# A second layer over pairs of blocks in seven products instead of eight, on one Trainium2 core

## The chip, the core and the metric

The kernel runs on one core of one Trainium2 chip. A core has five engines, each with an instruction queue of its own: TensorE (PE; loading a matmul's weights is recorded apart as PEld), VectorE (DVE), ScalarE (ACT), GpSimd (POOL) and SyncE (SP, which here only issues DMAs). The engines meet by semaphores. Each queue is worked in program order, so a waiting instruction holds everything behind it on its engine. The metric is the device time in microseconds, as the median of several runs.

## What is computed

```
x       = inputs x       (4, 6144, 256), f_logit the same shape, lower_bound (256,)
f       = lb + (1 - lb) * sigmoid(f_logit)
h[t]    = f[t] * h[t-1] + (1 - f[t]) * x[t]        # a scan over 6144 steps, h = y[t]
h1, h2  = y @ w1, y @ w2                           # 256 -> 1024
out     = maximum(h1, h2) @ w_out                  # 1024 -> 256, 24576 tokens
```

The kernel writes `maximum(h1, h2)` as `h1 + relu(h2 - h1)`. So the first layer is one product with `wd = w2 - w1` and a relu, and `h1 @ w_out` becomes `y @ w13` with `w13 = w1 @ w_out` made once. (The factor 1 - lb is taken out of the scan and put into `wd` and `w13`.)

## The kernel before

**Tiles.** The 24,576 tokens are cut into 48 blocks of 512 tokens (`TB`). The first four chunks hold one block each, the other 22 (chunks 4 to 25) two blocks (`CH` = 1024 tokens). D = 256 is two groups of 128 partitions (`KC` = 2), DFF = 1024 is eight (`FC` = 8).

**Getting data in.** From chunk 4 on, `fetch` (line 98, POOL) casts 1024 tokens of `f_logit` and of `x` from fp32 to bf16 into one of two DRAM scratches per tensor. `cross` (line 153, SP) then reads each scratch through a DMA transpose into `fT` or `xT` in SBUF, so that channels lie on partitions. The cast into a scratch waits until the transpose that last read that scratch has landed: f's waits for f's transpose, x's for x's. Chunks 1 to 3 are cast into SBUF and turned by TensorE instead (line 180). The very first block is loaded as fp32.

**The work of a block.** `gate(j)`: one sigmoid on ACT over 128x1024 (line 190). `scan_steps(j)`: two decays (line 209), one multiply (line 220) and two scans (line 233) on DVE. `first_layer(j, fc)`: two matmuls with 512 moving columns into one PSUM bank (line 381), then one relu of 128x512 on ACT (line 389). `second_layer(j, slot)`: for each of four token groups, two matmuls with `y` as weights and eight with `rt` as weights, 256 moving columns each (line 410), 40 matmuls to a block. DVE copies each pair of groups out of PSUM (line 430), and SP stores the block (line 433). The token groups are every fourth token, so the weights are read with a step of four elements.

**The order.** It is written out by hand. In iteration `j` of the main loop, eight slots hold `first_layer(j, fc)` and a part of `second_layer(j - 1, fc)` by turns, the gate and the scans of block j + 1 between them. `ahead` issues the transposes of a chunk when the loop is three blocks before it (`LEAD_CROSS`), and its casts seven blocks before. The gate of block j + 1 stands in iteration j, so chunk 5 (blocks 6 and 7) is first read by ACT in iteration 5.

Of the kernel before, what the change touches and what calls it, by code (L numbers as in the profile page):

```python
# [14 lines left out]
P = 128  # L15
# [3 lines left out]
def kernel(  # L19
# [18 lines left out]
    CH = 1024  # L38
    assert S % CH == 0
# [16 lines left out]
    def by_xbar(c, s):  # L56
        return c >= 4
# [6 lines left out]
    natpool = ctx.enter_context(tc.tile_pool(name="nat", bufs=6))  # L64
    inpool = ctx.enter_context(tc.tile_pool(name="inp", bufs=5))
    midpool = ctx.enter_context(tc.tile_pool(name="mid", bufs=2))
    ypool = ctx.enter_context(tc.tile_pool(name="ypool", bufs=4))
    rpool = ctx.enter_context(tc.tile_pool(name="rpool", bufs=2 * FC + 4))
    opool = ctx.enter_context(tc.tile_pool(name="opool", bufs=4))
    ps_t = ctx.enter_context(  # L70
        tc.tile_pool(name="ps_t", bufs=2, space=bass.MemoryType.PSUM)
    )
    ps_d = ctx.enter_context(
        tc.tile_pool(name="ps_d", bufs=3, space=bass.MemoryType.PSUM)
    )
    ps_o = ctx.enter_context(
        tc.tile_pool(name="ps_o", bufs=3, space=bass.MemoryType.PSUM)
# [4 lines left out]
        [dram.tile([CH, D], BF16, name=f"scr{s}_{q}") for q in range(NSCR)]  # L82
        for s in range(2)
    ]
    uses = [0, 0]
# [5 lines left out]
    def fetch(c):  # L91
        b, t0, nt, _ = chunks[c]
        for s in range(2):
            src = srcs[s][b, t0 : t0 + nt, :]
            if by_xbar(c, s):
                scr = scratch[s][uses[s] % NSCR]
                uses[s] += 1
                nc.gpsimd.dma_start(  # L98
                    out=scr[0:nt, :].rearrange("(p i) d -> p (i d)", p=P),
                    in_=src.rearrange("(p i) d -> p (i d)", p=P),  # L100
                )
                held[c, s] = scr
            else:
                nat = natpool.tile([P, CH // P, D], BF16, name=("fn", "xn")[s])
                nc.gpsimd.dma_start(
                    out=nat[:, 0 : nt // P, :].rearrange(
                        "p (k i) d -> p k (i d)", i=TB // P
                    ),
                    in_=src.rearrange(
                        "(k p i) d -> p k (i d)", p=P, i=TB // P  # L110
                    ),
                )
                held[c, s] = nat
# [3 lines left out]
    def fetch_first(k):  # L117
        nt = TB // 2
        for s in range(2):
            raw = const.tile([P, nt // P, D], FP32, name=f"raw{k}{s}")  # L120
            nc.sync.dma_start(  # L121
                out=raw[:],
                in_=srcs[s][0, k * nt : (k + 1) * nt, :].rearrange(
                    "(p i) d -> p i d", p=P
                ),
            )
            raws[k, s] = raw

    def first_bf16(k, s, copy):
        raw = raws[k, s]  # L130
        nat = const.tile([P, raw.shape[1], D], BF16, name=f"nat{k}{s}")
        copy(out=nat[:], in_=raw[:])
        raws[k, s] = nat

    def first_turn(k):
        nt = TB // 2
        for s in range(2):
            dst = ps_t.tile([P, KC, nt // P, P], BF16, name="tT")
# [9 lines left out]
    def cross(c):  # L148
        nt = chunks[c][2]
        for s in range(2):  # L150
            if by_xbar(c, s):
                dst = inpool.tile([P, KC, CH], BF16, name=("fT", "xT")[s])
                nc.sync.dma_start_transpose(  # L153
                    out=dst[:, :, 0:nt], in_=held[c, s][0:nt, :]
                )
                held[c, s] = dst

    def turn_steps(j):
        b, t0, nb, c, o = blocks[j]
        steps = []  # L160
        for s in range(2):
            if by_xbar(c, s):
                turned[j, s] = held[c, s][:, :, o : o + nb]
                continue
            dst = ps_t.tile([P, KC, TB], BF16, name="tT")
            ns = nb // P
            turned[j, s] = dst[:, :, 0:nb].rearrange("p k (i m) -> p k m i", i=ns)
            for q in range(ns):
                for h in range(KC):
# [3 lines left out]
                            held[c, s][:, o // P + q, h * P : (h + 1) * P],  # L173
# [9 lines left out]

    us = {}

    def gate(j):
        nb = blocks[j][2]
        u = midpool.tile([P, KC, TB], BF16, name="u")
        fT = turned[j, 0]
        nc.scalar.activation(  # L190
            out=like(u[:, :, 0:nb], fT), in_=fT, func=AF.Sigmoid, scale=-1.0
        )
        us[j] = u
# [6 lines left out]
    def scan_steps(j):  # L200
        b, t0, nb, c, o = blocks[j]
        u = us[j]
        ff = midpool.tile([P, KC, TB], BF16, name="ff")
        v = midpool.tile([P, KC, TB], BF16, name="v")
        y = ypool.tile([P, KC, TB], BF16, name="y")
        ys[j] = y

        def decay(h):
            nc.vector.tensor_scalar(  # L209
                out=ff[:, h, 0:nb],  # L210
                in0=u[:, h, 0:nb],
                scalar1=nom[:, h : h + 1],
                scalar2=1.0,
                op0=ALU.mult,
                op1=ALU.add,
            )

        def drive():
            xT = turned[j, 1]
            nc.vector.tensor_tensor(  # L220
                out=like(v[:, :, 0:nb], xT),
                in0=like(u[:, :, 0:nb], xT),
                in1=xT,
                op=ALU.mult,
            )

        def scan(h):
            if t0 == 0:
                init = 0.0
            else:  # L230
                pn = blocks[j - 1][2]
                init = ys[j - 1][:, h, pn - 1 : pn]
            nc.vector.tensor_tensor_scan(  # L233
                out=y[:, h, 0:nb],
                data0=ff[:, h, 0:nb],
                data1=v[:, h, 0:nb],
                initial=init,
                op0=ALU.mult,
                op1=ALU.add,
            )  # L240

        return [
            lambda: decay(0),
            lambda: decay(1),
            drive,
            lambda: scan(0),
            lambda: scan(1),
        ]

    first = {}  # L250

    def first_recurrence(k):
        nt = TB // 2
        cols = slice(k * nt, (k + 1) * nt)
        if k == 0:
            for t in ("u", "ff", "v"):
                first[t] = midpool.tile([P, KC, TB], BF16, name=t)
            ys[0] = ypool.tile([P, KC, TB], BF16, name="y")
        u, ff, v, y = (*(first[t] for t in ("u", "ff", "v")), ys[0])
        fT, xT = raws[k, 0], raws[k, 1]  # L260
        nc.scalar.activation(
            out=like(u[:, :, cols], fT), in_=fT, func=AF.Sigmoid, scale=-1.0
        )
        for h in range(KC):
# [7 lines left out]
            )  # L272
        nc.vector.tensor_tensor(
            out=like(v[:, :, cols], xT), in0=like(u[:, :, cols], xT), in1=xT,
            op=ALU.mult,
        )
        for h in range(KC):
# [13 lines left out]

    ident_f = const.tile([P, P], FP32)
# [8 lines left out]
    wdf = wpool.tile([P, KC, DFF], FP32)  # L301
    wd = wpool.tile([P, KC, DFF], BF16)
    w1T = wpool.tile([P, FC, D], BF16)
    w13 = wpool.tile([P, KC, D], BF16)
    NG = 2
    NQ = FC // NG
    w1n = [wpool.tile([P, KC, NQ * P], FP32, name=f"w1n{g}") for g in range(NG)]
    w2n = [wpool.tile([P, KC, NQ * P], FP32, name=f"w2n{g}") for g in range(NG)]
# [3 lines left out]

    def fcs(w, kc, g):
        return w[:, kc, g * NQ * P : (g + 1) * NQ * P].rearrange(
            "p (q m) -> p q m", q=NQ
        )
# [12 lines left out]
    def make_wd(fc, n):  # L329
        g, r = divmod(fc, NQ)  # L330
        qs = slice(r, r + n)
        cols = slice(fc * P, (fc + n) * P)
        nc.vector.tensor_tensor(  # L333
            out=wdf[:, :, cols].rearrange("p kc (q m) -> p kc q m", q=n),
# [4 lines left out]
        for kc in range(KC):  # L339
            if g == 0:  # L340
                nc.scalar.mul(wd[:, kc, cols], wdf[:, kc, cols], om[:, kc : kc + 1])  # L341
            else:
                nc.vector.tensor_scalar_mul(
                    out=wd[:, kc, cols], in0=wdf[:, kc, cols], scalar1=om[:, kc : kc + 1]
                )

    def turn_w1(k):
        g, r = divmod(k, NQ // 2)
        pt = ps_o.tile([P, KC, 2, P], FP32, name="psO")
# [11 lines left out]
    def make_w13():  # L361
        for kc in range(KC):
            psw = ps_o.tile([P, 2, D], FP32, name="psO")
# [9 lines left out]

    rts = {}

    def first_layer(j, fc):
        nb = blocks[j][2]
        y = ys[j]
        dT = ps_d.tile([P, TB], FP32, name="dT")
        for kc in range(KC):  # L380
            nc.tensor.matmul(  # L381
                dT[:, 0:nb],
                lhsT=wd[:, kc, fc * P : (fc + 1) * P],
                rhs=y[:, kc, 0:nb],
# [3 lines left out]
        rt = rpool.tile([P, TB], BF16, name="rt")  # L388
        nc.scalar.activation(out=rt[:, 0:nb], in_=dT[:, 0:nb], func=AF.Relu)  # L389
        rts[j, fc] = rt  # L390
# [3 lines left out]
    def second_layer(j, slot):  # L394
        b, t0, nb, c, o = blocks[j]
        ns = nb // P
# [3 lines left out]
        for k in range(slot * total // FC, (slot + 1) * total // FC):  # L400
            i, s = divmod(k, n)
            g, r = divmod(i, 2)
            if s == 0 and (r == 0 or j == NBLK - 1):
                acc["ps"] = ps_o.tile([P, 2, D], FP32, name="psO")
# [3 lines left out]
            left = y[:, s, i:nb:ns] if s < KC else rts[j, s - KC][:, i:nb:ns]  # L408
            right = w13[:, s, :] if s < KC else wob[:, s - KC, :]
# [8 lines left out]
            if j == NBLK - 1 and s == n - 1:  # L418
# [3 lines left out]
                r0 = b * S + t0  # L422
                (nc.sync if r else nc.scalar).dma_start(
                    out=out[r0 : r0 + nb, :].rearrange("(p n) d -> p n d", p=P)[
                        :, i : i + 1, :
# [21 lines left out]
    with tc.manual_schedule():  # L447
# [60 lines left out]
        if steps:  # L508
            gate(3)
# [62 lines left out]
```

## Time and profile before

| | us |
|---|---|
| Median of 3 runs (lowest, highest) | 400.92 (400.88, 401.1) |
| Span of the profiled execution | 428.3 |
| PE busy | 392.8 (92%) |
| PE's weight loads busy | 296.8 (69%) |
| ACT busy | 268.5 (63%) |
| DVE busy | 248.7 (58%) |
| POOL busy | 26.4 (6%) |
| Cast of f into scratch 0 or 1, median from issue to landing | 7.5 or 7.9 |
| Cast of x into scratch 0 or 1, the same | 12.4 or 13.6 |
| Store of a block (512 KB), the same | 4.8 |
| ACT idle before a gate until an f transpose had landed | 35.5 over 15 waits |
| PE idle before a first-layer matmul until a relu was done | 19.5 over 11 waits |

A time in the profile is that of one execution, the profiled one, which took about 27 us more than the runs that were timed. Busy is the time in which an engine has at least one instruction in work; instructions of one engine overlap at their ends, so the sum of their durations is larger. A matmul's recorded duration runs on after the next one has begun: the distance from start to start is what it costs. "Idle before" is the engine's idle time just in front of a group of instructions, with what ended it.

### The profile page before, as it was taken

To read this page: it belongs to the slowest core of one execution; us is meant where nothing else is said; L and a number is where in the kernel's file an instruction comes from. 1 tells how busy PE (TensorE), PEld (TensorE's weight loads), DVE (VectorE), ACT (ScalarE), POOL (GpSimd) and SP (SyncE) were. 2 spreads that over 40 slices of the span, in tenths; PEclk is the share of its full clock that TensorE was granted. 3 is DMA by queue.
4 is the path that set the end of the run, shared out by engine and by line. 5 is a ranking of instruction groups with operands and counts; after the bars stand their busy time and mean duration, and the time that the engine had idled before them with its cause. 6 is when DMAs were issued, how large, how long until landed. Compare 5 with 4: busy or idle time off the path is not lost.

```text
span 428.3 us, 6970 instructions
## 1 busy us (share of the span) xinstructions
PE 392.8 (92%) x2744; PEld 296.8 (69%) x2792; DVE 248.7 (58%) x359; ACT 268.5 (63%) x447; POOL 26.4 (6%) x58
## 2 busy tenths in 40 slices
PE   3999979798789999998997899999998999999996
PEld 1677756576557777776775577767676777777775
DVE  5785637455357566564653557657547656567551
ACT  3656656557366676675673666756657676776762
POOL 1400000000000000000000000000000000000000
PEclk9999999999989999999999699999999999999999
DMA  7999999999999999999998999999999999998112
GB/s 245 222 220 198 123 157 141 137 169 252 81 240 226 119 239 233 112 248 168 183 237 75 218 158 186 250 145 170 219 131 231 226 216 164 268 157 179 79 69 100
DMA packets 103377, 77.01 MB, mean 180 GB/s; under 512 B 93552, under 2 KB 94064, under 8 KB 102640
## 3 DMA queue, kind: packets, MB, share of 16 engines
q1 hardware_dynamic: 100512, 51.13, 66.7%
q0 software_dynamic: 2544, 25.17, 36.1%
q8 instruction: 22, 0.36, 0.4%
q10 hardware_dynamic: 288, 0.26, 0.2%
q14 instruction: 11, 0.09, 0.1%
HBM read 53.48 MB, written 48.23 MB: 237 GB/s over the span
## 4 chain that ended last, share of the span: by engine, by line
PE 46%; DMA 34%; SPq 15%; ACT 3%; DVE 1%; issue 1%; ACTq 0%
PE psO L410 25%; DMA fT<-scr_0_90 20%; PE dT L381 19%; SPq L153 13%; DMA fT<-scr_1_91 12%; ACT u L190 2%; DMA w1n_110<-in_moe_w_dram 2%; SPq L433 1%; PE psO L352 1%; ACT rt L389 1%; PE tT L180 1%; PE psO L365 0%; SPq L121 0%; DVE osb L430 0%; DVE y L233 0%
## 5 line engine op out<-in xcount | busy, mean ns | idle before, releaser
L389 ACT ACTIVATE rt<-dT 128x512 bf16<-128x512 f32 x384 | 219.2, 598 | 104.1 <-PE dT L381 100.0
L381 PE MATMUL dT<-y,wd 128*128 128x512 bf16 x720 | 219.5, 384 | 21.3 <-ACT rt L389 19.5
L410 PE MATMUL psO<-wob,rt 128*128 128x256 bf16 x1536 | 230.7, 274 | 2.7 <-issue 0.4
L410 PEld LDWEIGHTS <-rt 128*128 128x128 bf16 x1536 | 170.7, 114 | 41.4 <-issue 1.1
L233 DVE TENSOR_TENSOR_SCAN y<-ff,y,v 128x512 bf16<-128x512 bf16 x88 | 107.9, 1268 | 0.1
L430 DVE COPY osb<-psO 128x512 f32<-128x512 f32 x94 | 64.7, 690 | 59.0 <-PE psO L410 58.9
L381 PEld LDWEIGHTS <-wd 128*128 128x128 bf16 x768 | 75.8, 99 | 33.2 <-issue 24.6
L209 DVE TENSOR_SCALAR ff<-u,nom 128x512 bf16<-128x512 bf16 x94 | 29.0, 351 | 105.0 <-ACT u L190 105.0
L410 PE MATMUL psO<-w_109,y 128*128 128x256 bf16 x384 | 74.0, 275 | 0.0
L410 PEld LDWEIGHTS <-y 128*128 128x128 bf16 x384 | 43.4, 113 | 42.6 <-issue 3.5
L190 ACT ACTIVATE u<-fT 128x1024 bf16<-128x1024 bf16 x44 | 46.4, 1054 | 35.5 <-DMA fT<-scr_1_91 18.2
L220 DVE TENSOR_TENSOR v<-u,xT 128x1024 bf16<-128x1024 bf16 x44 | 30.3, 688 | 3.8 <-DMA xT<-scr_0_92 1.8
L98 POOL DMA_DIRECT2D scr_0_90<-in_f_logit_dram x11 | 5.4, 493 | 149.7 <-DMA fT<-scr_0_90 149.7
L98 POOL DMA_DIRECT2D scr_1_91<-in_f_logit_dram x11 | 5.3, 486 | 148.8 <-DMA fT<-scr_1_91 148.1
L233 DVE TENSOR_TENSOR_SCAN y<-ff,v 128x512 bf16<-128x512 bf16 x6 | 7.0, 1208 | 0.0
L98 POOL DMA_DIRECT2D scr_0_92<-in_x_dram x11 | 5.4, 488 | 18.7 <-DMA xT<-scr_0_92 16.9
L98 POOL DMA_DIRECT2D scr_1_93<-in_x_dram x11 | 5.3, 486 | 15.7 <-DMA xT<-scr_1_93 14.9
L190 ACT ACTIVATE u<-tT 128x1024 bf16<-128x1024 bf16 x3 | 3.2, 1058 | 4.3 <-PE tT L180 4.3
L352 PE MATMUL psO<-ident_f,w1n_110 128*128 128x128 f32 x8 | 1.9, 422 | 3.4 <-DMA w1n_110<-in_moe_w_dram 3.4
L341 ACT ACTIVATE wd<-wdf,om 128x128 bf16<-128x128 f32 (+1 forms) x6 | 2.2, 428 | 4.3 <-DVE wdf L333 4.3
L352 PEld LDWEIGHTS psO<-ident_f,w1n_110 128*128 128x128 f32 x8 | 1.6, 221 | 3.7 <-issue 3.7
L220 DVE TENSOR_TENSOR v<-u,tT 128x1024 bf16<-128x1024 bf16 x3 | 3.6, 1216 | 0.0
(49 smaller groups left out, 45.1 us busy)
## 6 DMA issues: line engine op xcount, KB each, us to landing
out_dram<-osb SPq DMA_DIRECT2D x47, 512.0 KB, 4.8
scr_0_90<-in_f_logit_dram POOLq DMA_DIRECT2D x11, 512.0 KB, 7.5
scr_0_92<-in_x_dram POOLq DMA_DIRECT2D x11, 512.0 KB, 12.4
scr_1_91<-in_f_logit_dram POOLq DMA_DIRECT2D x11, 512.0 KB, 7.9
scr_1_93<-in_x_dram POOLq DMA_DIRECT2D x11, 512.0 KB, 13.6
fn<-in_f_logit_dram POOLq DMA_DIRECT2D x3, 256.0 KB, 7.9
xn<-in_x_dram POOLq DMA_DIRECT2D x3, 256.0 KB, 8.6
w2n_112<-in_moe_w_dram SPq DMA_DIRECT2D x1, 512.0 KB, 6.5
```

The lines of the kernel that those rows point to most:

```text
L98: nc.gpsimd.dma_start(out=scr[0:nt, :].rearrange("(p i) d -> p (i d)", p=P), in_=src.rearrange("(p i) d -> p (i d)", p=P),)
L153: nc.sync.dma_start_transpose(out=dst[:, :, 0:nt], in_=held[c, s][0:nt, :])
L180: nc.tensor.transpose(dst, src, ident[:])
L190: nc.scalar.activation(out=like(u[:, :, 0:nb], fT), in_=fT, func=AF.Sigmoid, scale=-1.0)
L209: nc.vector.tensor_scalar(out=ff[:, h, 0:nb], in0=u[:, h, 0:nb], scalar1=nom[:, h : h + 1], scalar2=1.0, op0=ALU.mult, op1=ALU.add,)
L220: nc.vector.tensor_tensor(out=like(v[:, :, 0:nb], xT), in0=like(u[:, :, 0:nb], xT), in1=xT, op=ALU.mult,)
L233: nc.vector.tensor_tensor_scan(out=y[:, h, 0:nb], data0=ff[:, h, 0:nb], data1=v[:, h, 0:nb], initial=init, op0=ALU.mult, op1=ALU.add,)
L352: nc.tensor.transpose(pt[:, kc, q, :], half(w1n, g)[:, kc, 2 * r + q], ident_f[:])
L381: nc.tensor.matmul(dT[:, 0:nb], lhsT=wd[:, kc, fc * P : (fc + 1) * P], rhs=y[:, kc, 0:nb], start=(kc == 0), stop=(kc == KC - 1),)
L389: nc.scalar.activation(out=rt[:, 0:nb], in_=dT[:, 0:nb], func=AF.Relu)
L410: nc.tensor.matmul(ps[:, r, :], lhsT=left, rhs=right, start=(s == 0 and (r == 0 or j == NBLK - 1)), stop=(s == n - 1 and (r == 1 or j == N ...
L430: nc.vector.tensor_copy(out=osb[:, 2 * g : 2 * g + 2, :], in_=ps[:])
```

## The change

**The product.** Blocks 2p and 2p + 1 form a pair. The product of their relu outputs (1024 tokens, 1024 channels) with `w_out` (1024 x 256) is seen as a product of 2x2 block matrices: tokens by block, channels in two halves of four groups (`HC` = `KH` = 4), output columns in two halves of 128 (`lo`, `hi`). It is done in seven block products instead of eight, in Winograd's form. Each product is 4 token groups x 4 channel groups = 16 matmuls with 128 moving columns; the four results take 8 more matmuls each for `y @ w13`. A pair thus has 144 matmuls with 128 columns where it had 80 with 256. Blocks 0 to 3, and 46 and 47, keep `second_layer`; the 21 pairs from blocks 4 and 5 to blocks 44 and 45 use `sevenths`.

**Around it.** Four sums of relu outputs per pair (128x2048 bf16 each, DVE) feed three products and a fourth. PSUM banks are kept and added on to, with three copies of them into SBUF ("snapshots", ACT). Three of the four results leave by an add of a bank and a snapshot (DVE), the fourth by a copy (ACT). Five small differences of weights are made once (`make_sevens`, DVE).

**First layer.** Its PSUM tile holds two channel groups (two banks), two tiles instead of three of one bank, and one relu does both, 128x1024. The relu writes its result in token-group order, so that the weights of the products lie contiguously; those with `y` keep the step of four.

**Recurrence.** Gates and decays work on a pair: four sigmoids of 128x512 (`pair_gate`) two pairs ahead, two decays of 128x1024, two multiplies and four scans (`pair_scans`) one pair ahead.

**Data.** Still two scratches per tensor and whole chunks. After `cross(c)` has issued both transposes, POOL reads one element of each result (`pool_waits`), and only then issues both casts of chunk c + 2. The first five chunks are cast at the start. The transposes of the chunk of pair p + 3 are issued at slot 2 of pair p.

```diff
+    HC = 4
...
     def by_xbar(c, s):
-        return c >= 4
+        return chunks[c][2] == CH
+
+    PAIR0 = 2
+    NPAIR = NBLK // 2
+    KH = FC // 2
...
-    inpool = ctx.enter_context(tc.tile_pool(name="inp", bufs=5))
+    inpool = ctx.enter_context(tc.tile_pool(name="inp", bufs=4))
...
-    rpool = ctx.enter_context(tc.tile_pool(name="rpool", bufs=2 * FC + 4))
+    ypool = ctx.enter_context(tc.tile_pool(name="ypool", bufs=7))
+    rpool = ctx.enter_context(tc.tile_pool(name="rpool", bufs=10))
+    spool = ctx.enter_context(tc.tile_pool(name="spool", bufs=5))
+    snpool = ctx.enter_context(tc.tile_pool(name="snpool", bufs=5))
...
     def cross(c):
...
+        if c >= NCHUNK:
+            return
         for s in range(2):
+            dst = inpool.tile([P, KC, CH], BF16, name=("fT", "xT")[s])
+            nc.sync.dma_start_transpose(out=dst[:], in_=scratch[s][c % NSCR][:])
+            held[c, s] = dst
+        if c + NSCR < NCHUNK:
+            for s in range(2):
+                pool_waits(held[c, s][:, 0, 0:1])
+            for s in range(2):
+                fetch(c + NSCR, s)
...
     def first_layer(j, fc):
...
+        if fc % 2:
+            nc.scalar.activation(
+                out=rts[j, k][:, g - 1 : g + 1, :].rearrange(
+                    "p q (i m) -> p q i m", m=P
+                ),
+                in_=dT[:].rearrange("p q (m i) -> p q i m", m=P),
+                func=AF.Relu,
+            )
...
+    def sum_of(p, name, a, b, op):
+        t = spool.tile([P, HC, TB], BF16, name="S")
+        nc.vector.tensor_tensor(out=t[:], in0=a, in1=b, op=op)
+        sums[p, name] = t
...
+        product("X", part(0, 0), lambda k: wob[:, k, lo], True)
+        then(snapshot("X", 1))
+        product("B", part(0, 1), lambda k: wob[:, KH + k, lo], True)
+        linear("B", ja, lo, False)
+        then(leave("B", ja, lo, 1, False))
+        product("X", sub(2), lambda k: t2[:, k, :])
+        then(snapshot("X", 2))
+        product("E", sub(1), lambda k: t1[:, k, :], True)
+        then(snapshot("E", 5))
+        product("X", sub(3), lambda k: t3[:, k, :])
+        linear("X", jb, hi, False)
+        then(leave("X", jb, hi, 5, False))
+        product("E", sub(4), lambda k: wob[:, KH + k, hi])
+        linear("E", ja, hi, False)
+        then(leave("E", ja, hi, 2, True))
+        product("X", part(1, 1), lambda k: t4[:, k, :])
+        linear("X", jb, lo, True)
+        then(leave("X", jb, lo, None, True))
...
+        cross(5)
+        early = scan_steps(3)
+        for fc in range(FC):
+            second_layer(1, fc)
+            if fc < 3:
+                early[fc]()
+            if fc % 2:
+                pair_gate(PAIR0, fc // 2)
...
+        for fc in range(FC):
+            first_layer(3, fc)
+            second_layer(2, fc)
+            if fc % 2:
+                pair_gate(PAIR0 + 1, fc // 2)
...
+            if fc == 0:
+                cross(6)
+
+        for p in range(PAIR0, NPAIR):
...
+                seq += [
+                    (0, scans["decay"]),
+                    (10, scans["drive0"]),
+                    (40, scans["scan00"]),
+                    (52, scans["scan01"]),
+                    (76, scans["drive1"]),
+                    (84, scans["scan10"]),
+                    (104, scans["scan11"]),
+                    (124, lambda: sum3(p)),
+                ]
+            if not first:
+                seq += [
+                    (4, lambda: sum2(p - 1)),
+                    (20, lambda: sum1(p - 1)),
+                    (64, lambda: sum4(p - 1)),
+                ]
...
+            gates = {5: 0, 11: 1, 13: 2, 15: 3} if p + 2 < NPAIR else {}
+            for slot in range(2 * FC):
+                first_layer(2 * p + slot // FC, slot % FC)
...
+                upto = (slot + 1) * len(steps) // (2 * FC)
+                for step in steps[done_steps:upto]:
+                    step()
+                done_steps = upto
+                while seq and seq[0][0] < (slot + 1) * 9:
+                    seq.pop(0)[1]()
+                if slot == 2 and p + 3 < NPAIR:
+                    cross(blocks[2 * p + 6][3])
+                if slot in gates:
+                    pair_gate(p + 2, gates[slot])
+        for j in (NBLK - 2, NBLK - 1):
+            for slot in range(FC):
+                second_layer(j, slot)
```

A pair has 16 slots. In each, TensorE gets two first-layer matmuls of pair p and nine steps of the products of pair p - 1; `part(t, k)` is the relu output of block t and channel half k, and `sub(n)` the n-th sum.

## The prediction

> **What bounds the kernel now.** I read the busy shares first, then the costliest groups, the timeline of TensorE, and last the transfers. Of a group, the figures behind the bar are busy us and mean ns of one, then idle us in front of it with what ended it.
>
> ```profile
> L389 ACT ACTIVATE rt<-dT 128x512 bf16<-128x512 f32 x384 | 219.2, 598 | 104.1 <-PE dT L381 100.0
> L381 PE MATMUL dT<-y,wd 128*128 128x512 bf16 x720 | 219.5, 384 | 21.3 <-ACT rt L389 19.5
> L410 PE MATMUL psO<-wob,rt 128*128 128x256 bf16 x1536 | 230.7, 274 | 2.7 <-issue 0.4
> L430 DVE COPY osb<-psO 128x512 f32<-128x512 f32 x94 | 64.7, 690 | 59.0 <-PE psO L410 58.9
> ```
>
> ACT and DVE wait for TensorE (100.0 and 58.9 us), and TensorE waits little: it is the bound. The timeline of TensorE (start, length, line) gives its price per matmul, as start-to-start distance:
>
> ```profile
> 21.10 0.61 PE L180 MATMUL tT<-ident,fn 128*128 128x128 bf16 x8
> ...
> 21.99 0.38 PE L410 MATMUL psO<-w_109,y 128*128 128x256 bf16 x2
> ...
> 26.36 0.61 PE L180 MATMUL tT<-ident,fn 128*128 128x128 bf16 x8
> ...
> 40.44 0.38 PE L410 MATMUL psO<-w_109,y 128*128 128x256 bf16 x2
> ...
> 48.25 0.38 PE L410 MATMUL psO<-w_109,y 128*128 128x256 bf16 x2
> ```
>
> Sixteen matmuls of 128 columns, each with weights of its own: (21.99 - 21.10)/16 = 0.0556 us. Forty of 256 columns: (26.36 - 21.99)/40 = 0.109 us. A whole block: 48.25 - 40.44 = 7.81 us, so one of 512 columns is (7.81 - 40 x 0.109)/16 = 0.215 us.
>
> The main loop has 45 such iterations (blocks 3 to 47), 351.5 us. In the profile they took 380, from 40.0 until 419.97, where the last block's second layer starts. So 28.5 us of the span of 428.3 are waits, begun by late `fT` (the chain of waits gives 34% to DMA). Without them the span is 399.8, and the median of 400.92 is that plus 1.1 around it. **The timed runs thus show no such wait: they are TensorE from end to end**, and I build the forecast on 400.9.
>
> **What the change does to TensorE.** A pair was 2 x 7.81 = 15.62 us. Now it is 32 x 0.215 for the first layer and 144 x 0.0556 = 8.01 us for seven products and the `y` terms: 14.89. Gain 0.73 us a pair, over 21 pairs **15.3 us**: 385.6. The saving of columns is 10% (18,432 for 20,480), as the `y` terms are not saved.
>
> The rule against this: the Trainium skill, "TensorE: Matmul & The Clock Gate", section "Back-to-back issue gap", says that in a real stream of weight loads and matmuls 128 columns sustain about 81 ns, since both set the spacing. By it a pair is 6.88 + 144 x 0.081 = 18.54 us, 2.92 more than before, and the kernel takes 462. The break-even is (15.62 - 6.88)/144 = 0.0607. The row above is such a stream, at full granted clock, 16 long, at 0.0556, so I take the row. The stepped weights (32 of 144) were loaded just as densely behind those transposes; I add nothing. Ends: 0 and, at 81 ns for those 32 alone, 0.8 us a pair, which would eat the gain.
>
> **DVE and ACT, each beside TensorE.** From the timelines of one undisturbed block (start, length):
>
> ```profile
> 142.62 0.62 DVE L209 TENSOR_SCALAR ff<-u,nom 128x512 bf16<-128x512 bf16 x2 [1.38 <-ACT u L190]
> 143.15 0.69 DVE L220 TENSOR_TENSOR v<-u,xT 128x1024 bf16<-128x1024 bf16 x1
> 144.46 0.69 DVE L430 COPY osb<-psO 128x512 f32<-128x512 f32 x1 [0.62 <-PE psO L410]
> 145.06 2.45 DVE L233 TENSOR_TENSOR_SCAN y<-ff,y,v 128x512 bf16<-128x512 bf16 x2
> ```
>
> ```profile
> 141.04 0.60 ACT L389 ACTIVATE rt<-dT 128x512 bf16<-128x512 f32 x1 [0.38 <-PE dT L381]
> 141.53 1.05 ACT L190 ACTIVATE u<-fT 128x1024 bf16<-128x1024 bf16 x1
> 142.48 1.08 ACT L389 ACTIVATE rt<-dT 128x512 bf16<-128x512 f32 x2
> ```
>
> An instruction starts some 0.1 us before its forerunner ends: copy to scan 0.60, multiply 0.60, scan 1.19, relu of 512 0.49, gate of 1024 0.95.
> - ACT per pair: eight relus of 1024 at 0.95, four gates of 512 and four bank copies at 0.49 = 11.5 us.
> - DVE per pair: four scans 4.77, two multiplies 1.2, two decays of 1024 about 0.83 (0.265 each, plus 0.15 by the slope from the 256-wide form, 276 ns, to 351), three adds, four sums. A sum has twice the elements of the multiply (688 ns). The multiplies on turned data give a fixed part of 0.15 us (684 ns for 512, 1216 for 1024), so 1.22 long, 1.13 in a row; ends 1.13 and 1.38.
> - An add reads a PSUM bank and an fp32 snapshot, 512 elements. The only fp32 two-tensor row of that size (L333) took 1074 ns. The skill's "VectorE: DVE Perf Modes", section on the trn2 errata, gives (N + 151)/0.96 = 691 ns. L333 reads both with a step of four; the copy from PSUM (690) is nearer to it, so 0.69, 0.60 in a row. DVE is then 13.1 us, or with L333's price 14.3, both under 14.89.
>
> Both engines are covered in sum. In order, it is tight: the last gate of a pair stands behind slot 15's relu (ready about 14.6) and the last bank copy, so it ends near 16.7, 1.8 us into the next pair, and DVE's first instruction there, the decay, waits for it. From 1.8: second sum done at 3.9, first 5.6, fourth 9.8, bank X emptied 12.2, all done 15.1, before the next 16.7. TensorE asks for these at 4.4, 6.1, 10.0 and 12.65. **The margin is 0.2 to 0.5 us**, so I cost these waits at nothing; with L333's price the fourth sum and bank X come some 0.3 late, 21 x 0.3 = 6 us. The relus have at least 0.7 us before their PSUM tile is wanted, with two tiles instead of three. Weight differences: five DVE instructions of about 0.4 beside blocks 2 and 3, hidden by DVE's idle time.
>
> **Transfers.** The same bytes. In steady state the transposes go out 19 slots (17.7 us) before their first gate, against two blocks (15.6) before. They no longer share the DMAs with casts issued when f's transpose alone had landed; f's cast waits for x's transpose, 1.3 to 2.8 us more by POOL's waits, covered by a whole pair of lead. SP has no new wait; POOL's two small reads hold only casts.
>
> At the **start** the lead shrinks. The gates of chunk 5 move from iteration 5 (56 us) to the stage of block 3 (first wanted at about 41.8), on ACT, in front of relus; chunk 6's from 72 to about 52. POOL's casts show when f's transposes of chunks 4 and 5 had landed:
>
> ```profile
> 36.98 0.49 POOL L98 DMA_DIRECT2D scr_0_90<-in_f_logit_dram  x1 [17.67 <-DMA fT<-scr_0_90]
> 60.98 0.49 POOL L98 DMA_DIRECT2D scr_1_91<-in_f_logit_dram  x1 [20.41 <-DMA fT<-scr_1_91]
> ```
>
> Chunk 5 at 60.5 would hold TensorE 19 us; but timed runs lose nothing with it wanted at 56, so at most 14. From below: SP is free at 35.9 and the shortest landing of an f transpose is 7.2 us: 43.1, a wait of 1.3. Chunk 6 by the same rows: casts after 48 - 7.5, transposed by 55.4, wanted at 53.4: 2.0. I take the lower end, 3.3 us, as the timed runs are those without late transfers: 385.6 + 3.3 = **389**.
>
> **Rivals.**
> 1. *Half is given back* (0.21): chunk 5 or 6 late by 5 to 11 us, or DVE's chain at 0.3 to 0.5 us a pair: 394 to 400. For it: thin margins, 15 us less lead. Against it: timed runs without a DMA wait.
> 2. *Slower: the loop through the scratch* (0.15). Transposes of c, casts of c + 2, transposes of c + 2 now run strictly one after the other, both tensors together: two pairs cost T + C. By the profile T = 7.8 (SP held by f's issue) + 9.3 (x landing) = 17.1, C = 13.6 + 0.5: 31.2, 15.6 a pair, which with the start's 3.3 is about 404. It decides from T + C = 31.2. For it: these are the profile's medians. Against it: those transposes ran beside casts; the shortest are 7.2 and 5.1, which gives T + C of 26, 13 a pair.
> 3. *81 ns* (under 0.01): 462, against the row.
>
> **The numbers.** Likeliest (0.60): 389, own range 385 to 393. What a measurement of this kernel can tell from no change is 0.2%, 0.8 us; 0.04 for that. Faster 0.81, slower 0.15. The range, 384.5 to 400, leaves out rival 2 and little else.
>
> **What would show it.** About 3,000 matmuls of 128 columns 0.056 apart; a pair in 14.9 us; sums near 1.22, relus of 1024 near 1.05, adds near 0.69. Wrong it is if TensorE waits for a sum or a bank each pair, if DVE idles less than 1 us a pair, if first-layer matmuls between 40 and 60 us wait for relus held by a gate, or if casts land after their transposes are wanted.

## The result, and the profile after

The changed kernel took 395.71 us (median of 4 runs, 393.6 to 398.24) against 401.01 before: ratio 0.9873, 95% interval 0.9824 to 0.9923. Two further sets of six runs gave 393.65 and 393.47 (ratios 0.9792, 0.9761 to 0.9824, and 0.9796, 0.9765 to 0.9826). So the gain is 5 to 8 us where I forecast 12. To read what follows one must know that the profile of the kernel before is of a late execution (span 428.3), that about one in four of its runs takes 410 us or more, and that the ratios leave such runs out, of both kernels.

From the page of the changed kernel, the groups that answer to those shown of before (behind the bar busy us and mean ns, then idle us in front):

```profile
L432 ACT ACTIVATE r<-dT 128x1024 bf16<-128x1024 f32 x192 | 196.5, 1026 | 75.4 <-PE dT L424 74.3
L424 PE MATMUL dT<-y,wd 128*128 128x512 bf16 x768 | 229.2, 386 | 7.4 <-ACT r L432 7.4
...
L602 PE MATMUL ps<-t,S 128*128 128x128 bf16 x1008 | 77.0, 219 | 0.3 <-issue 0.3
...
L493 DVE TENSOR_TENSOR S<-r 128x2048 bf16<-128x2048 bf16 x42 | 51.1, 1217 | 4.9 <-ACT r L432 4.9
...
L560 DVE TENSOR_TENSOR osb<-ps,sn 128x512 f32<-128x512 f32 x63 | 42.9, 681 | 8.9 <-ACT r L432 5.4
```

One relu of 128x1024 costs 1026 ns where two of 128x512 cost 2 x 598. A sum of 128x2048 takes 1217 ns, an add of bank and snapshot 681. TensorE waits 7.4 us for relus, three times in all, and for no sum and no bank.

The windows of the changed kernel (window, its length, then busy us of PE, PEld, DVE, ACT and POOL with instruction counts, the granted clock, DMA share, GB/s) say where:

```profile
20.00:40.00 20.00, 16.61 (x149) 12.66 (x147) 15.75 (x21) 9.71 (x13) 0.72 (x3) 0.98 1.09 200
40.00:60.00 20.00, 19.40 (x109) 11.57 (x109) 13.83 (x21) 12.73 (x15) 2.25 (x6) 0.85 1.12 213
60.00:80.00 20.00, 16.56 (x153) 11.22 (x153) 13.88 (x16) 13.81 (x18) 3.83 (x8) 0.91 1.15 234
80.00:100.00 20.00, 20.00 (x241) 15.10 (x239) 17.61 (x21) 16.34 (x22) 2.08 (x5) 1.00 1.08 215
98.88:113.83 14.95, 14.95 (x180) 11.22 (x178) 13.21 (x16) 11.98 (x17) 1.59 (x5) 1.00 1.07 219
```

From 80 us on TensorE is busy with hardly a gap: one later pair takes 15.4 us, the others 14.95. The last window is as long as one pair: 14.95 us, with DVE 13.21 and ACT 11.98 us busy. Between 20 and 80 us it has gaps, and the granted clock falls to 0.85 and 0.91. Nearly all of the loss is at the start. The timeline of TensorE there (start, length, line, count, and in brackets the idle time before):

```profile
35.83 1.03 PE L424 MATMUL dT<-y,wd 128*128 128x512 bf16 x4
40.57 4.42 PE L424 MATMUL dT<-y,wd 128*128 128x512 bf16 x10 [3.71 <-ACT r L432]
44.79 0.63 PE L471 MATMUL ps<-w,y 128*128 128x256 bf16 x2
45.22 0.84 PE L471 MATMUL ps<-wob,r 128*128 128x256 bf16 x3
```

Block 2's first layer stops after eight matmuls (the first line is the last four of them), when both PSUM tiles are full, and waits 3.71 us for a relu. Then the next ten matmuls of 512 columns, eight of block 2 and two of block 3, need 4.2 us, 0.42 each instead of 0.216. The granted clock is 0.51 there, in the window from 39 to 44. The relu was held on ACT by the gate of chunk 4, the first line of ACT's timeline below. The second wait is the gate of chunk 6, which waited 3.63 us for its transpose, with two relus right behind it; TensorE waited 3.47 us there, and the granted clock from 64 to 69 is 0.75:

```profile
37.42 2.19 ACT L273 ACTIVATE u<-fT 128x512 bf16<-128x512 bf16 x4 [5.57 <-DVE y L218]
...
61.84 0.63 ACT L273 ACTIVATE u<-fT 128x512 bf16<-128x512 bf16 x1 [3.63 <-DMA fT<-scr]
62.38 1.92 ACT L432 ACTIVATE r<-dT 128x1024 bf16<-128x1024 f32 x2
```

The view puts the 5.57 us down to DVE's scan of block 3, which ended at 37.3, just when f landed. The scan is not the cause: in c1 the same gate began at 35.56, before that scan was done, and in e2 at 40.83, long after it, each time as f landed.

POOL's timeline shows when transposes land (`waited`: POOL reads one element of the result) and when casts go out:

```profile
37.45 0.18 POOL L337 CAST waited<-fT 128x1 f32<-128x1 bf16 x1 [19.56 <-DMA fT<-scr]
...
39.65 0.58 POOL L100 DMA_DIRECT2D scr<-in_f_logit_dram  x1 [0.32 <-issue]
...
47.27 0.18 POOL L337 CAST waited<-fT 128x1 f32<-128x1 bf16 x1 [6.57 <-DMA fT<-scr]
...
52.00 0.49 POOL L100 DMA_DIRECT2D scr<-in_f_logit_dram  x1
...
61.86 0.69 POOL L337 CAST waited<-fT 128x1 f32<-128x1 bf16 x1 [8.89 <-DMA fT<-scr]
...
64.19 0.49 POOL L100 DMA_DIRECT2D scr<-in_f_logit_dram  x1 [0.26 <-issue]
```

f of chunk 4 lands at 37.4, of chunk 5 at 47.3, of chunk 6 at 61.9. The first load of first-layer weights of a block gives the stages. "Nothing lost" is e6's block 4 plus a pair-2 stage of 11.24 us, worked out from 32 x 0.215 and 40 x 0.109 (the shortest measured, in e3, is 11.17).

| First-layer start, us | block 3 | block 4 (pair 2) | block 6 (pair 3) |
|---|---|---|---|
| Nothing lost (e6; pair 3 worked out) | 38.42 | 46.41 | 57.65 |
| Changed kernel, run shown here (span 396.1) | 43.51 | 52.65 | 68.92 |
| Changed kernel, c1 (span 388.2) | 40.27 | 48.60 | 60.35 |
| Changed kernel, c2 (span 391.8) | 42.55 | 50.88 | 65.02 |

The run shown here loses 11.3 us before pair 3, c2 7.4 and c1 2.7; c1's span is 7.9 shorter. In these three traces the start makes the scatter; of c1's slowest run, 408.66, there is no trace.

### The profile page after: what moved, and what is told of

Read it like the earlier page. It is cut to its first block, busy times and chain, and to the rows that moved or that the text cites. A ratio compares the mean times of both kernels' runs of the same rounds, so it can differ in the third digit from the quotient of the medians.

```text
span 396.1 us, 9570 instructions
## 1 busy us (share of the span) xinstructions
PE 378.3 (96%) x4136; PEld 279.4 (71%) x4136; DVE 321.7 (81%) x383; ACT 288.5 (73%) x383; POOL 41.7 (11%) x98
## 4 chain that ended last, share of the span: by engine, by line
PE 85%; DMA 3%; ACT 1%; issue 0%; DVE 0%; ACTq 0%
PE ps L602 43%; PE dT L424 39%; PE ps L471 3%; DMA fT<-scr 3%; ACT r L432 0%; ACT u L273 0%; DVE osb L480 0%; ACTq L273 0%
## 5 line engine op out<-in xcount | busy, mean ns | idle before, releaser
L432 ACT ACTIVATE r<-dT 128x1024 bf16<-128x1024 f32 x192 | 196.5, 1026 | 75.4 <-PE dT L424 74.3
L602 PEld LDWEIGHTS <-S 128*128 128x128 bf16 x1344 | 89.2, 98 | 34.7
L602 PEld LDWEIGHTS <-r 128*128 128x128 bf16 x1008 | 66.9, 98 | 27.3
L602 PE MATMUL ps<-t,S 128*128 128x128 bf16 x1008 | 77.0, 219 | 0.3 <-issue 0.3
L273 ACT ACTIVATE u<-fT 128x512 bf16<-128x512 bf16 x88 | 54.8, 626 | 9.2 <-DVE y L218 5.6
L493 DVE TENSOR_TENSOR S<-r 128x2048 bf16<-128x2048 bf16 x42 | 51.1, 1217 | 4.9 <-ACT r L432 4.9
L493 DVE TENSOR_TENSOR S<-r,S 128x2048 bf16<-128x2048 bf16 x42 | 50.8, 1209 | 0.9 <-ACT r L432 0.9
L602 PE MATMUL ps<-wob,r 128*128 128x128 bf16 x672 | 51.2, 219 | 0.0
L560 DVE TENSOR_TENSOR osb<-ps,sn 128x512 f32<-128x512 f32 x63 | 42.9, 681 | 8.9 <-ACT r L432 5.4
L602 PE MATMUL ps<-w,y 128*128 128x128 bf16 x504 | 48.7, 219 | 0.0
L471 PEld LDWEIGHTS <-r 128*128 128x128 bf16 x192 | 19.2, 100 | 4.3 <-issue 0.5
```

Of the source, the lines that this page charges most:

```text
L273: nc.scalar.activation(out=mids[p + NBLK, "u"][:, h, cols], in_=held[c, 0][:, h, cols], func=AF.Sigmoid, scale=-1.0,)
L432: nc.scalar.activation(out=rts[j, k][:, g - 1 : g + 1, :].rearrange("p q (i m) -> p q i m", m=P), in_=dT[:].rearrange("p q (m i) -> p q i ...
L471: nc.tensor.matmul(ps[:, r, :], lhsT=left, rhs=right, start=(s == 0 and (r == 0 or j == NBLK - 1)), stop=(s == n - 1 and (r == 1 or j == N ...
L493: nc.vector.tensor_tensor(out=t[:], in0=a, in1=b, op=op)
L560: nc.vector.tensor_tensor(out=dst, in0=bank[b][:], in1=snap[name][:], op=ALU.add)
L602: nc.tensor.matmul(bank[b][:, i, :], lhsT=a, rhs=w, start=fresh, stop=after is not None, skip_group_check=True,)
```

## The experiments

Theory S: the loss is the start, where transposes come later than the gates want them. Rival M: a pair costs more than worked out. Later a theory T came in: casts beside a transpose starve it, that is, make it land late.

**c1, c2: the changed kernel again**, without an edit.

> The changed kernel again, as the neighbour of the next runs: 393.6 to 398.2 as before.

> The changed kernel once more as neighbour: 393 to 396, single runs from 390 to 409 by how the first transposes fall.

Measured: 393.65 (390.38 to 408.66) and 393.47 (390.51 to 394.57). TensorE's timeline of c2, at the first wait:

```profile
40.99 1.94 PE L424 MATMUL dT<-y,wd 128*128 128x512 bf16 x8 [3.98 <-ACT r L432]
43.17 0.59 PE L424 MATMUL dT<-y,wd 128*128 128x512 bf16 x2 [0.25 <-ACT r L432]
```

The wait is longer than in the run above, 3.98 us, but the granted clock behind it stays at 1.00, and the ten matmuls run at 0.216 us. So the half clock does not follow every such wait.

**e1: chunk 4's gates behind block 2's relus.**

```diff
         for fc in range(FC):
             second_layer(1, fc)
             if fc < 3:
                 early[fc]()
-            if fc % 2:
-                pair_gate(PAIR0, fc // 2)
         early[3]()
         for fc in range(FC):
             first_layer(2, fc)
+        for q in range(4):
+            pair_gate(PAIR0, q)
```

> The changed kernel with the four gates of chunk 4 moved behind the relus of block 2 on ACT; nothing else differs. Theory S (the gain was lost at the start, where a gate that waits for a transpose holds relus, and TensorE then runs at half clock for a while): the 3.7 us wait before block 2's fifth first-layer matmul goes, and the half clock behind it; the first pass of seven-product pairs begins some 4 to 6 us earlier, unless the gate of chunk 6 then waits by as much longer, as its transpose lands at 61 to 62 us whatever TensorE does. So 390 to 392 if the gain stays, 395 to 396 if chunk 6's wait takes it all. Rival M (a pair is slower than worked out): no change, 395 to 396, and a pair still over 14.9 us.

Measured: 392.89 (391.34 to 394.71), ratio 0.9781 (0.9706 to 0.9856). Block 3 begins at 38.8 instead of 43.5, so the first wait and its half clock are gone. But block 4 begins at 52.2, hardly earlier than 52.7. ACT's timeline of e1 shows why, the wait of chunk 5's gate, then of chunk 6's:

```profile
47.21 0.63 ACT L273 ACTIVATE u<-fT 128x512 bf16<-128x512 bf16 x1 [3.92 <-DMA fT<-scr]
...
58.61 0.63 ACT L273 ACTIVATE u<-fT 128x512 bf16<-128x512 bf16 x1 [0.85 <-DMA fT<-scr]
```

The wait has moved to chunk 5, whose f lands at 47.2, as in the run shown above (47.3; in c1 it was 42.3). Chunk 6's shrank from 3.63 to 0.85. The time lies a little above what I gave for a gain that stays, and is within the scatter of c1 and c2. A pair is still 14.95, against M.

**e2: a third scratch per tensor, six chunks cast at the start.**

```diff
-    NSCR = 2
+    NSCR = 3
...
-        for c in range(1, 6):
+        for c in range(1, 7):
```

> The changed kernel with three scratches per tensor instead of two, and six chunks cast at the start, so that chunk 6's casts do not wait for chunk 4's transposes. Theory S: chunk 6 is transposed some 8 us earlier, the wait of 3.5 us at 60 us goes, and the half clock behind it: about 390. If the extra cast at the start delays chunk 4's transposes instead, the first wait grows and the time stays at 394 to 397. Rival M: no change.

Measured: 400.53 (395.57 to 412.61, 20 runs), ratio 0.9923 (0.9899 to 0.9947): worse than the changed kernel. POOL's and TensorE's timelines of e2, which are those of its fastest run:

```profile
40.85 0.18 POOL L337 CAST waited<-fT 128x1 f32<-128x1 bf16 x1 [20.59 <-DMA fT<-scr]
```

```profile
43.97 4.29 PE L424 MATMUL dT<-y,wd 128*128 128x512 bf16 x10 [6.90 <-ACT r L432]
```

Chunk 4's f lands at 40.8 instead of 37.4, and the wait is 6.9 us instead of 3.7. TensorE doesn't wait at chunk 6. Of the two outcomes that I had written down it is the second, and it overshot it. Chunk 4's f lands later than in any other trace of this start (35.1 to 38.0): an added cast seems to push back the transposes in front of it, the first hint of T. What the slower runs lost is in no trace.

**e3: eight products of 256 columns in the changed kernel.**

```diff
-            steps = [] if first else sevenths(p - 1)
+            steps = []
...
+                if not first:
+                    second_layer(2 * p - 2 + slot // FC, slot % FC)
```

The entries of `sum1` to `sum4` are left out of `seq`.

> The changed kernel with its data path, relus, gates and scans, but each pair's second layer as eight products with 256 moving columns, as before the change; no sums, snapshots or adds. Theory S: a pair costs 15.62 us again instead of 14.95, 21 x 0.67 = 14 us more: 408 to 410, slower than the kernel before, as the start's waits stay. Rival M: the product form gave little, so 397 to 400.

Measured: 407.72 (404.98 to 412.61), ratio 1.0127 (1.0053 to 1.02). Its pairs start 15.64 us apart; one of them:

```profile
104.96:120.60 15.64, 15.64 (x114) 11.17 (x112) 9.62 (x13) 10.26 (x12) 1.33 (x4) 1.00 1.12 231
```

15.64 against 14.95. So the product is worth 0.69 us a pair, 21 x 0.69 = 14.5 us (the medians differ by 12.0 from the first set of the changed kernel and by 14.1 from c1's), and the rest of the change, without it, makes the kernel slower than before. M falls.

**e4: f's cast as soon as f's transpose has landed.**

```diff
             for s in range(2):
                 pool_waits(held[c, s][:, 0, 0:1])
-            for s in range(2):
                 fetch(c + NSCR, s)
```

> The changed kernel, but f's cast of chunk c + 2 goes out as soon as f's transpose of chunk c has landed, before x's. Theory S: chunk 6's f cast goes out 2 us earlier (37.5 instead of 39.7), but beside x's transpose; chunk 6 wanted 3.5 us too late gains 1 to 2 us at best: 394 to 396. A rival on transfers (casts beside a transpose starve it, so that the rule of both transposes is worth much): transposes of x land several us later in every pair, TensorE waits in steady state, and the time is 400 or more.

Measured: 452.21 (423.11 to 455.68), far beyond the 394 to 396 of theory S; its profiled run, the fastest of the four, has a span of 421.0. Most pairs still take 14.9 us, but others up to 24.4. SP's timeline and POOL's, for one chunk of e4:

```profile
119.11 10.27 SPq L150 DMA_TRANSPOSE fT<-scr  x1
```

```profile
118.91 0.49 POOL L100 DMA_DIRECT2D scr<-in_f_logit_dram  x1
...
137.33 1.28 POOL L336 CAST waited<-fT 128x1 f32<-128x1 bf16 x1 [16.20 <-DMA fT<-scr]
```

SP issues f's transpose at 119.11, 0.2 us behind a cast. It holds SP for 10.3 us and lands at 137.3, 18 us later. The expectation had this rival and its mark, 400 or more. So "once both have landed" is no detail: the seven-product kernel depends on it.

**e6: that rule alone, in the kernel before** (with the first five chunks cast at the start, as in the change).

```diff
     def cross(c):
...
+        if by_xbar(c, 0) and c + NSCR < NCHUNK:
+            for s in range(2):
+                pool_waits(held[c, s][:, 0, 0:1])
+            fetch(c + NSCR)
...
-        done["fetch"] = done["cross"] = 1
-        ahead("fetch", fetch, 4)
+        done["cross"] = 1
+        for c in range(1, 6):
+            fetch(c)
...
-            ahead("fetch", fetch, j + LEAD_FETCH)
```

> The kernel before the change with one part of the change: both casts of chunk c + 2 go out when both transposes of chunk c have landed, and the first five chunks are cast at the start. Theory T (casts let go beside a transpose starve the next transposes; the rule alone keeps the transfers at some 12 us a chunk): the median stays at 400 to 401, as TensorE bounds it, but runs of 410 to 450 no longer occur, and a profiled run has a span below 402 instead of 428. Rival: the rule is worth something only with the changed lead of the transposes; runs above 410 stay.

Measured: 400.51 (13 runs, all within 400.08 to 401.27), ratio 0.9991 (0.9982 to 0.9999), span 398.4; the 19 runs of the kernel before beside it went from 400.5 to 437.66. From issue to landing, median us, in e6, where SP issues a chunk's transposes every 15.6 us:

```profile
fT<-scr SPq DMA_TRANSPOSE x22, 6.2
xT<-scr SPq DMA_TRANSPOSE x22, 4.5
```

6.2 and 4.5 against some 15.8 and 9.3 before the change (in its late execution; of one without late transfers there is no trace). Had one run in four still been late, 13 without one would be luck of about 2% (0.75 to the 13th). The rule makes the kernel before steady and hardly faster, as TensorE bounds it. T holds.

**e5: all early gates behind relus.** On top of e1:

```diff
-            if fc % 2:
-                pair_gate(PAIR0 + 1, fc // 2)
+            if fc == FC - 1:
+                for q in range(4):
+                    pair_gate(PAIR0 + 1, q)
...
+                if first:
+                    if slot == 2 * FC - 1:
+                        for q in range(4):
+                            pair_gate(p + 2, q)
-                if slot in gates:
+                elif slot in gates:
                     pair_gate(p + 2, gates[slot])
```

> All gates of the start moved behind relus: chunk 4's behind block 2's, chunk 5's behind block 3's, chunk 6's behind the last relu of pair 2. Theory S: all waits of TensorE for a held relu between 35 and 65 us go and with them the half clock; pair 3 begins near 58 us instead of 69, or 1 us later as DVE's first instruction there waits for chunk 6. So 11 us less than the profiled 396.1 of the changed kernel: a span of 384 to 386, 386 to 388 timed. A rival: the same lateness comes back on DVE, which needs the gates for the scans, and y is late for the first layer of pair 2 or 3 instead: 390 to 393.

Measured: 393.97 (390.75 to 397.72), no better than c1 beside it. Pair 3 begins at 59.8, somewhat later than the 58 or 59 expected. But the next three pairs take 15.8, 16.7 and 15.6 us. POOL's timeline of e5, f of chunks 7 and 8:

```profile
67.32 1.12 POOL L337 CAST waited<-fT 128x1 f32<-128x1 bf16 x1 [1.44 <-DMA fT<-scr]
...
84.18 1.33 POOL L337 CAST waited<-fT 128x1 f32<-128x1 bf16 x1 [6.56 <-DMA fT<-scr]
```

They were wanted at slot 5 of pairs 3 and 4, at 64.4 and 80.3 (start of the pair, 59.8 or 75.6, plus 5 x 0.934, a sixteenth of 14.95). The lateness came back, not on DVE as the rival had it, but at the next gates. So here, as in e1, where a gate stands on ACT decided only where the late transfer was paid.

**e7: TensorE kept busy in the first wait.** Sixty transposes of the identity go into a bank that nothing reads.

```diff
             first_layer(2, fc)
+            if fc == 3:
+                idle = ps_o.tile([P, TB // P, P], BF16, name="ps")
+                for q in range(60):
+                    nc.tensor.transpose(idle[:, q % 4, :], ident[:], ident[:])
```

> The changed kernel with 60 transposes of the identity (3.3 us) put on TensorE where it waits for chunk 4's gate, before block 2's fifth channel group; the output is the same. Theory S with half clock: the wait stays (relus are held as before), but the ten 512-column matmuls behind it run at 0.216 us each instead of about 0.43, so pair 2 begins 2 to 3 us earlier than 52.8. If the slow matmuls there come from something else (the weights, the relus), they stay slow.

```profile
37.83 2.56 PE L692 MATMUL ps<-ident 128*128 128x128 bf16 x43
40.57 1.94 PE L424 MATMUL dT<-y,wd 128*128 128x512 bf16 x7 [0.17 <-ACT r L432]
42.76 0.59 PE L424 MATMUL dT<-y,wd 128*128 128x512 bf16 x2 [0.25 <-ACT r L432]
```

The matmuls go on at the same 40.57, but at 0.216 us and a granted clock of 1.00; block 3 begins 1.4 us earlier (42.1), pair 2 1.8 us (50.9), less than the 2 to 3 I gave. So the clock, not the work, made them slow. But that the filling kept the clock up is not shown: c2, with nothing filled in and a wait of 3.98 us, ran them as fast and began pair 2 at the same 50.9. The one timed run, 396.83, says nothing on this, as it lost time at later gates.

**e8: later gates in pairs 3 to 5 too.** On top of e5:

```diff
+            if p in (3, 4, 5):
+                gates = {11: 0, 12: 1, 13: 2, 15: 3}
```

> As e5, and in pairs 3 to 5 the gates of two pairs later stand at slots 11 to 15 instead of 5 to 15. Theory S (the transfers start late and come 12.1 us apart, so they catch up with a pair of 14.95 by only 2.85 us each; in e5 the lateness of chunks 7 to 9 came back in pairs 3 to 5, at 15.8, 16.7 and 15.6 us): these pairs fall to at most 15.3, pair 3 begins before 61 us, and the time is 389 to 391. Rival (what is lost in pairs 3 to 5 is DVE's chain, whatever the gates' place): they stay near 16, 393 to 395.

Measured: 394.67 (388.72 to 404.56), ratio 0.9719 (0.9692 to 0.9747). Three runs of the six, 388.72 to 391.30, fall into the 389 to 391 or beside it; the other three take 398 to 405. In its trace, of a run of 391.30, pairs 3 to 7 took 16.1, 14.95, 14.95, 15.6 and 16.1: the lateness came back once more, later. By its median it missed, and it left the scatter: moving gates doesn't settle it.

**e9: no cast beside f's next transpose.** On top of e8:

```diff
-        if c + NSCR < NCHUNK:
-            for s in range(2):
-                pool_waits(held[c, s][:, 0, 0:1])
-            for s in range(2):
-                fetch(c + NSCR, s)
+        if c > 4 and c - 1 + NSCR < NCHUNK:
+            pool_waits(held[c - 1, 1][:, 0, 0:1])
+            pool_waits(held[c, 0][:, 0, 0:1])
+            for s in range(2):
+                fetch(c - 1 + NSCR, s)
```

> As e8, and chunk c + 1's casts wait for x's transpose of chunk c - 1 and for f's transpose of chunk c, so that f's transpose never runs beside casts. Theory S: f of chunks 6 and 7 lands some 3 to 6 us earlier (55 and 67 us in every run instead of 55 to 62 and 66 to 71), the start loses at most 3 us, 388 to 390, and runs scatter less. Against it: the casts start later by the time of f's transpose, some 3 us a chunk; if a cast is then not done when its transpose is wanted, pairs grow over 15 us in steady state and the time is 395 or more.

Measured: 389.02 (388.78 to 389.39), ratio 0.9698 (0.9686 to 0.971). It beats both kernels in every run. Medians of its transposes, then POOL's waits for f of chunks 6 and 7:

```profile
fT<-scr SPq DMA_TRANSPOSE x22, 6.0
xT<-scr SPq DMA_TRANSPOSE x22, 4.4
```

```profile
53.84 0.62 POOL L337 CAST waited<-fT 128x1 f32<-128x1 bf16 x1 [9.74 <-DMA fT<-scr]
...
67.03 1.05 POOL L337 CAST waited<-fT 128x1 f32<-128x1 bf16 x1 [11.02 <-DMA fT<-scr]
```

f of chunk 6 lands at 53.8 instead of 61.9 (c1 54.8, c2 59.4), and the median landing of f is 6.0 us instead of 12.1 (c1 10.0, c2 11.6). Pair 3 begins at 59.4 and takes 15.8 us, the others 14.95.

**e10: that cast rule alone on the changed kernel**, gates where the change put them.

> The changed kernel with the cast rule of e9 alone; all gates where the change put them. Theory S: chunk 6's f lands near 54 as in e9, so the wait at 60 us and most of the scatter go; chunk 4's gate still holds block 2's relus, for 3 to 6 us with the half clock behind it, and chunk 5's a little: e9's 389.0 plus 3 to 6, 392 to 395, scatter under 2 us. If the moved gates gave nothing in e9, 389 to 390.

Measured: 389.35 (388.97 to 390.86), ratio 0.9714 (0.969 to 0.9739): outside the 392 to 395 that I gave to S, inside what I wrote for gates that give nothing. ACT's timeline of e10, chunk 4's gates and chunk 6's:

```profile
35.14 2.19 ACT L273 ACTIVATE u<-fT 128x512 bf16<-128x512 bf16 x4 [3.01 <-DMA fT<-scr]
...
55.11 0.63 ACT L273 ACTIVATE u<-fT 128x512 bf16<-128x512 bf16 x1 [1.37 <-DMA fT<-scr]
```

The waits are 3.0 and 1.4 us, TensorE's longest wait for a relu is 1.2, and the granted clock from 30 to 70 is 1.00. So the cast rule, with no other edit, takes 4 to 6 us off the changed kernel, and moving the gates adds nothing that can be told. That chunk 4's f landed at 35.1 here, and between 35.4 and 38.0 in other runs of the same start, is not explained by any edit; why is open.

## Why the prediction was wrong

**Right: the bound and the price of a pair.** A pair came to 14.95 us where the sum gave 14.89; matmuls of 128 columns stand 0.0567 us apart (nine in 0.51 us), not at the 81 ns of the Trainium skill. DVE's 13.1 and ACT's 11.5 us came to 13.21 and 11.98. (The runs of the kernel before stand 1.8 us above their span, not 1.1, so its span without waits is 399.1, not 399.8; the forecast, built on the timed 400.9, does not move by it.) The add took 681 ns in the mean, near the 691 of the rule, not L333's 1074. The chain with its margin of 0.2 us held: no wait for a sum or a bank in the run shown (in c1 one of 1.0 us for a snapshot, while ACT was held by a late gate).

**Wrong: the step "Transfers", its part on the start, the term of 3.3 us.** The run profiled lost 11.3 us before pair 3, c1 2.7 and c2 7.4. With this in place of the 3.3, 21 x 0.06 us for the pairs and what single later pairs lost (0.6, 1.3 and 0.2 us), 385.6 becomes 398.7, 390.8 and 394.4; these runs were timed at 398.24, 390.38 and 393.91, so the sum closes. By the medians the start cost 7 to 9 us. Three things in the term failed.
- Chunk 4 was left out. Its gates had moved too, from 41.2 to about 32, and the quoted row put its landing just before 36.98. That alone was 3.7 us of waiting, in front of all else. Chunk 5, which I charged with 1.3, cost nothing behind it. Chunk 6 waited 3.63, not 2.0. (c1, where chunk 4 came at 35.6 and chunk 6 at 54.8, shows that the lower end can happen; to forecast by it was to count on luck.)
- "I take the lower end", the shortest landing of 7.2 us, with the reason that the timed runs show no late transfers. They show it for chunk 4's gate at 41.2 and for chunk 5's at 56 us and the later ones; for these gates at 32 to 52 they show nothing. The profile's own landing of chunk 4, which lay at hand, went unused.
- A wait of TensorE was costed at its own length. Behind 3.71 us the clock was halved, some 1.8 us more (pair 2 began at 52.65, and at 50.9 in e7 and c2 with the full clock); the granted clock of 0.75 from 64 to 69 shows the same at the second wait. The Trainium skill's "TensorE: Matmul & The Clock Gate", Part 1, gives about 3.4 us of idleness as what drops the clock; the trace agrees, with 3.71 us of idleness and a granted clock of 0.51 in the window from 39 to 44. But c2's wait of 3.98 us left the clock at 1.00, so idleness of that length doesn't always do it.

**Missed: what the casts' new wait is worth.** I had it cost nothing for its lead, and made the strict loop through the scratch the slower rival, at 15.6 us a chunk. Measured, a round is 12.1 at the start: casts of f go out at 39.65, 52.00 and 64.19, (64.19 - 39.65)/2 = 12.3, and over four rounds to 88.14 12.1. The old order is the slow one (e4, e6). I did say that transposes no longer share the DMAs with such casts, and gave it no number.

**The rivals.** The first, half given back by late chunks at 394 to 400, is what happened, by its DMA branch alone (the two further sets lie just under 394). That no run of 385 to 386 came is due to the start even in e9, which loses 1.8 us before pair 3 and 0.9 in it. These 2.7 us are near the 3.3 of my term, and e9's 389.02 is near the 389: the term was about right for a start whose transposes are mostly clear of casts, and the change had no such start.

## What to carry to other kernels

When a change asks for data earlier, work out the first few loads one by one, each landing against its new due time, and reckon with a half clock behind a wait of more than 3 us on TensorE (it came behind ten of the twelve in the traces here). On a queue that waits in order, moving the waiting instruction only moves the wait: the late transfer itself has to come earlier. Let a transpose that someone waits for go before casts whose lead is long, and hold the casts until it has landed.

## What the runs showed of the hardware

**Casts slow transposes.** The same transpose of f took, in the median, 6.0 us from issue to landing mostly kept apart from casts (e9; 6.1 in e10), 12.1 with casts let go soon after it (the changed kernel), and 14.6 with casts let go just before it (e4), where one issue for f held SP for up to 10.3 us (median 7.9), in e9 for up to 6.8 (median 3.4). Medians of the changed kernel and of e4:

```profile
fT<-scr SPq DMA_TRANSPOSE x22, 12.1
xT<-scr SPq DMA_TRANSPOSE x22, 9.7
```

```profile
fT<-scr SPq DMA_TRANSPOSE x22, 14.6
xT<-scr SPq DMA_TRANSPOSE x22, 9.4
```

The transposes' packets are 256 bytes (90,112 of them in the trace), the casts' bulk goes in packets of 32 KB (704). That the sizes are the reason is argued, not shown. A plain sharing of the DMA engines explains a part: by the packet records, the casts' 32-KB packets took some 43% of the engines' time while f's transposes of the changed kernel were under way, and 24% in e9. As an estimate, 12.1 and 6.0 us less that share leave 6.9 and 4.6, so it is not the whole.

**A half clock behind some waits.** Behind 3.71 us of idleness ten matmuls took twice their time (0.42 for 0.216 us, granted clock 0.51); behind 3.98 us in c2 the same ten took 0.216 at a granted clock of 1.00. Of the twelve waits of TensorE of more than 3 us that the traces have behind their first 30 us, ten have a lower granted clock right behind them; the other two are c2's and one of 3.72 us in e4. What decides it is not shown. In e7 the clock stayed up with the wait filled by unused work, but c2 shows that it can stay up without.
